# Loading q and k once, on the two partition halves of one tile, and filling the other operand planes by DMAs within SBUF

## The chip, the cores and the metric

The kernel runs on one core of one Trainium2 chip. The metric is the device time of one execution in microseconds, from the core's own records; it is quoted as the median of several executions. The core has TensorE (PE, matmuls, with its weight loads PEld), VectorE (DVE), ScalarE (ACT), GpSimd (POOL) and SyncE (SP), which issues nearly all DMAs here and runs each queue in order.

## The reference

Two layers follow each other, in float32 throughout.

```python
# attention: B=8, H=8, S=576, D=64
scores = matmul(q, k.T) / sqrt(D)
cum = cumsum(log(clip(f, 1e-4, 1)), axis=-1)
scores = where(causal, -1e9, scores + cum[:, None] - cum[None, :])
attn = exp(scores - max) / (sum + 1e-9)
x = matmul(attn, v)                     # reshaped to 4608 tokens x 512
# feed forward: 512 -> 2048 -> 512
h = x @ w_in
out = (max(h, 0) + log1p(exp(-|h|))) @ w_out
```

Matmuls of float32 operands are costly, so most of them are made from operands that are split in two: a rounded part ("hi", type fp32r) and the rest ("lo"). A product is then hi·hi + hi·lo + lo·hi.

## The kernel before, in words

The work is 68 attention jobs and ten feed-forward blocks of tokens (two of 256, eight of 512). Jobs 0 to 11 belong to the first batch and use unsplit float32 operands (the "plain" path, `load32`). Jobs 12 to 67 are 56 heads, eight for each of the other seven batches, and use split operands; only they are touched by the change. While attention runs, feed-forward matmuls of blocks that are ready are put between its matmuls; when the last head is done, about 200 us of feed-forward are left.

The order of the instructions of each engine is written by a planner (`Plan`, L48). It holds estimated costs and latencies of every operation, places the one that can start first, picks an engine where two are allowed (`copies`, L194: ACT or DVE; `scales`, L199: DVE, ACT or POOL), and emits it. Each engine, and SP's queue, then runs its list in that order on the chip and waits where an operand is late. Buffers come from pools with a fixed number each (`BUFS`, L252).

For one head of the split path:

- `load` (L669): two DMAs (L673) bring q and k, transposed to 64 partitions, into the tile `raw`, once on partitions 0 to 63 and once on 64 to 127. Each DMA carries both q and k, 288 KB. There is one `raw` buffer, so the load of a head waits until the head before has done with it.
- `prepare` (L694) fills `T`, a tile of four planes of 576 columns. There are two of them; a head's `T` comes free when the scores of the head two before it are done.
  - plane 0: q hi, on both halves (`q_hi`, a cast at L211)
  - plane 1: q lo on the lower half (`q_lo`, L718), constants and decay rows above it
  - plane 2: k hi on the lower half, k lo on the upper (`k_hi`, a cast at L211; `k_lo`, L712)
  - plane 3: k hi on the lower half (`k_hi2`, a DMA within SBUF, L709), constants and decay rows above it
  - the decay rows come by two small DMAs from DRAM (L702, L703)
- scores (L756, L757): for each of six pieces, one matmul of plane 0 by plane 2 over 128 partitions (q hi·k hi and q hi·k lo at once) and one of plane 1 by plane 3 over 68 partitions (q lo·k hi and the decay).
- then the row minimum with the mask (DVE, L761), the exponential (ACT, L781), the reciprocal of the sum (DVE, L794), the scaling of the weights (`scale`, L803 on ACT, L805 on POOL or DVE), the transposes (PE, L852), the split of the weights (L211 and L871) and the product with v (PE, L911).

Of the kernel before, what the change touches and what calls it, by code (L numbers as in the profile page):

```python
# [12 lines left out]
F32R = mybir.dt.float32r  # L13
# [34 lines left out]
class Plan:  # L48
# [120 lines left out]
def on_act(n, more=0.0, psum=False):  # L169
    return On("ACT", (0.067 if psum else 0.095) + n / 1200 + more)  # L170
# [16 lines left out]
NO_ENGINE = On("", 0.0)  # L187
# [6 lines left out]
def copies(n):  # L194

    return [on_act(n), on_dve(n, True, bias=COPY_BIAS)]
# [8 lines left out]
def subs(n):  # L205

    return on_dve(n, port=True)


def copy(e, out, in_):  # L210
    (e.tensor_copy if hasattr(e, "tensor_copy") else e.copy)(out, in_)  # L211
# [3 lines left out]
def tile_decay_attention_softplus_ffn(  # L215
# [18 lines left out]
    B, D, H, _, S = qkT.shape  # L234
    NT, DM = out.shape
    DFF = w_in.shape[1]
    P = 128
# [7 lines left out]
    BH = B * H  # L245
# [4 lines left out]
    QF, QR = [(0, 128), (128, 128)], [(256, 64), (320, 128), (448, 128)]  # L250

    BUFS = dict(T=2, att=4, h=2, acc=2, fe=4, ph=3, pl=3, ph64=2, gh=LAG + 1, gl=LAG + 1, xh=1, xl=1,  # L252
                x32=2, wl=2, vhl=3, vraw=1, raw=1)
    plan = Plan(BUFS | dict(T0=4, stat=4, p=2, xh0=1, xh1=1, xl0=1))
    add, give = plan.add, plan.give

    def add_dma(emit, kb, n=1, eng="SP", **more):
        return add(on_dma(kb, n, eng), emit, lag=dma_lag(kb, n, eng), **more)
# [9 lines left out]
    def buf(tag, shape, name, dtype=F32):  # L268
        return pool.tile(shape, dtype, tag=tag, name=name, bufs=BUFS[tag])
# [9 lines left out]
    T = {}  # L279
# [79 lines left out]
    def decay():  # L359
        box = {}  # L360

        def load(e):
            box["f"] = buf("wl", [P, 1024], "fs")[0:BH, 0:S]
            e.dma_start(out=box["f"], in_=f)

        def clip(e):
            e.tensor_scalar(box["f"], box["f"], 1e-4, 1.0, ALU.max, ALU.min)

        def log(e):
            e.activation(box["f"], box["f"], AF.Ln)  # L370

        def scan(e):

            c = cum[0] = buf("x32", [P, NCC, S], "cum")[0:BH, 0, :]
            x = box["f"][:, 0:256]
            e.tensor_tensor_scan(c[:, 0:256], x, x, 0.0, ALU.add, ALU.min)

        def scan_rest(e):
            c = cum[0]
            x = box["f"][:, 256:S]  # L380
            e.tensor_tensor_scan(c[:, 256:S], x, x, c[:, 255:256], ALU.add, ALU.min)

        def split(e):
            hl = buf("raw", [P, 2, S], "chl", F32R)
            ch, cl = box["hl"] = hl[0:BH, 0, :], hl[0:BH, 1, :]
            e.tensor_copy(ch, cum[0])
            e.tensor_sub(cl, cum[0], ch.bitcast(F32))

        def store(e):
            for r in range(2):  # L390
                e.dma_start(out=aug_d[:, r, :], in_=box["hl"][r].bitcast(F32))

        o = add_dma(load, BH * S / 256, takes=("wl",))
        o = add(on_dve(S, True), clip, after=[o])
        l = add(on_act(S), log, after=[o])
        decay_ready["first"] = add(On("DVE", 0.63), scan, after=[l], takes=("x32",))
        c = decay_ready["sums"] = add(On("DVE", 0.78), scan_rest, after=[decay_ready["first"]])
        give("wl", [c])
        def rest(after):
            s = add(On("DVE", 1.05, 0.0, True), split, after=[c, *after], takes=("raw",))  # L400
            w = add_dma(store, BH * S / 128, 2, after=[s] + first_rows)
            give("raw", [add(NO_ENGINE, mark, after=[w])])
            decay_ready["rows"] = w
            cum_used.append(s)

        return rest
# [168 lines left out]
    def attention(job):  # L575

        b, heads = job["b"], job["heads"]
# [90 lines left out]

        def load():  # L669
            def qk(e):  # L670
                raw = buf("raw", [P, 2, S], f"raw{n}")
                for i in range(2):
                    e.dma_start(out=raw[64 * i : 64 * i + 64], in_=qkT[b, :, heads[0]])  # L673
                st["raw"] = raw[:, 0, :], raw[:, 1, :]

            st["qk"] = add_dma(qk, 576, 2, takes=("raw",))

        def split_v():
            def v_hi(e):
# [14 lines left out]
        def prepare():  # L694
            def begin(e):
                nonlocal t, tb, qA, qB, kA, kB
                t = T[number % 2]
                tb = t.bitcast(F32)
                qA, qB, kA, kB = (t[:, i, :] for i in range(4))

            def decay_rows(e):
                e.dma_start(out=tb[64:66, 1, qs:qe], in_=aug_d[bh][:, qs:qe])  # L702
                e.dma_start(out=tb[66:ST, 3, :], in_=aug_d[bh])  # L703

            def k_hi(e):
                copy(e, t[:, 2, :], st["raw"][1])

            def k_hi2(e):
                e.dma_start(out=tb[0:64, 3, :], in_=tb[0:64, 2, :])  # L709

            def k_lo(e):
                e.tensor_sub(t[top, 2, :], st["raw"][1][top], tb[top, 2, :])  # L712

            def q_hi(e):
                copy(e, t[:, 0, qs:qe], st["raw"][0][:, qs:qe])

            def q_lo(e):
                e.tensor_sub(t[0:64, 1, qs:qe], st["raw"][0][0:64, qs:qe], tb[0:64, 0, qs:qe])  # L718

            split_v()  # L720
            if number < nplain + 2:
                set_rows(number % 2, T0_end[2 * (number % 2)] + T0_end[2 * (number % 2) + 1])
            start = add(NO_ENGINE, begin, after=T_set[number % 2], takes=("T",), lag=0.0)
            a = add_dma(decay_rows, 9, 2, after=[start, decay_ready["rows"]])
            kh = add(copies(S), k_hi, after=[start, st["qk"]])
            qh = add(copies(qe - qs), q_hi, after=[start, st["qk"]])
            kh2 = add_dma(k_hi2, 144, after=[kh])
            kl = add(On("DVE", 0.79, 0.0, True), k_lo, after=[kh])
            ql = add(subs(qe - qs), q_lo, after=[qh])
            give("raw", [kl, ql])  # L730
            st["T"] = [a, kl, ql, kh2]


        def stat_tile(ti):
# [236 lines left out]
        def loads():  # L971
# [5 lines left out]
            s=[lambda ti=ti: stat_tile(ti) for ti in range(nt)],  # L977
            w=[lambda bi=bi: weights(bi) for bi in range(len(banks))],
# [485 lines left out]
```

## Time and profile before

| | before |
|---|---|
| median of 3 runs | 1197.46 us (1197.27 to 1198.01) |
| span of the profiled execution | 1196.2 us |
| busy PE / PEld | 1177.1 / 969.0 us |
| busy DVE / ACT / POOL | 851.4 / 852.5 / 140.3 us |
| granted TensorE clock | 1.000 |
| moved by DMAs | 172.01 MB |
| scores of split heads run from / to | 135.3 / 988.4 us |

The span is read from the first to the last instruction of one execution; the median stands 1.26 us above it. A busy PE is not a PE at its peak, since its matmuls overlap and their ends are modelled: idle time that shows between them is a floor for what PE lost. The page's idle columns say how long an engine stood still just before a group of instructions, and what ended most of that.

### The profile page before, as it was taken

To read this page: it belongs to the slowest core of one execution; us is meant where nothing else is said; L and a number is where in the kernel's file an instruction comes from. 1 tells how busy PE (TensorE), PEld (TensorE's weight loads), DVE (VectorE), ACT (ScalarE), POOL (GpSimd) and SP (SyncE) were. 2 spreads that over 40 slices of the span, in tenths; PEclk is the share of its full clock that TensorE was granted. 3 is DMA by queue.
4 is the path that set the end of the run, shared out by engine and by line. 5 is a ranking of instruction groups with operands and counts; after the bars stand their busy time and mean duration, and the time that the engine had idled before them with its cause. 6 is when DMAs were issued, how large, how long until landed. Compare 5 with 4: busy or idle time off the path is not lost.

```text
span 1196.2 us, 19275 instructions
## 1 busy us (share of the span) xinstructions
PE 1177.1 (98%) x6122; PEld 969.0 (81%) x6122; DVE 851.4 (71%) x2085; ACT 852.5 (71%) x2033; POOL 140.3 (12%) x143
## 2 busy tenths in 40 slices
PE   8999999999999999999999999999999999999998
PEld 6666678878888888888888888888888888888887
DVE  7998999897787778777787778677867773223322
ACT  6676888888886778678777778688867773444543
POOL 3200011111111110102011101011111110000000
PEclk9999999999999999999999999999999999999999
DMA  7855655545555645655565546555465524211210
GB/s 215 255 171 162 183 152 155 131 135 155 143 160 166 177 131 147 182 162 155 143 187 158 147 130 187 149 162 147 146 181 151 156 81 136 89 36 53 88 53 35
DMA packets 107317, 172.01 MB, mean 144 GB/s; under 512 B 20256, under 2 KB 77616, under 8 KB 107216
## 3 DMA queue, kind: packets, MB, share of 16 engines
q1 hardware_dynamic: 107200, 170.78, 50.1%
q8 instruction: 48, 0.79, 0.3%
q14 instruction: 53, 0.43, 0.1%
q10 hardware_dynamic: 16, 0.01, 0.0%
HBM read 126.49 MB, written 35.95 MB: 136 GB/s over the span
## 4 chain that ended last, share of the span: by engine, by line
PE 77%; DVE 12%; ACT 4%; DMA 3%; issue 2%; POOL 1%; SPq 0%; DVEq 0%; POOLq 0%; ACTq 0%
PE h L1069 27%; PE acc L1154 27%; PE b L852 7%; PE o L911 5%; PE s L756 3%; PE s L757 3%; DVE s L761 2%; PE h L1050 2%; PE acc L1173 1%; POOL p L805 1%; ACT p L781 1%; DMA raw<-in_qkT 1%; PE s L754 1%; PE o L905 1%; DVE T L712 1%
## 5 line engine op out<-in xcount | busy, mean ns | idle before, releaser
L1069 PE MATMUL h<-xh,wih 128*128 128x512 f32 (+1 forms) x576 | 229.1, 401 | 0.0
L781 ACT ACTIVATE p<-s,negm 128x288 f32<-128x288 f32 (+7 forms) x384 | 182.6, 478 | 55.0 <-DVE negm L761 53.4
L1069 PE MATMUL h<-xl,wih 128*128 128x512 f32 (+1 forms) x576 | 216.8, 379 | 0.0
L805 POOL TENSOR_SCALAR p<-p,rsum 64x64 f32<-64x64 f32 (+4 forms) x106 | 119.1, 1133 | 742.9 <-DVE rsum L794 292.5
L1116 DVE SCALAR_TENSOR_TENSOR h<-h,e 128x512 f32<-128x512 f32 x136 | 95.1, 699 | 138.1 <-ACT e L1108 137.3
L761 DVE CUSTOM_DVE_ANT_0 s<-s,cmask 128x288 f32<-128x288 f32 (+5 forms) x320 | 137.2, 439 | 74.1 <-PE s L757 63.6
L1102 ACT ACTIVATE e<-h 128x512 f32<-128x512 f32 x144 | 85.4, 594 | 112.7 <-PE h L1069 106.8
L1154 PE MATMUL acc<-woh_dt_float32r,gh 128*128 128x512 f32 x376 | 153.1, 407 | 0.1
L1069 PE MATMUL h<-xh,wl 128*128 128x512 f32 (+1 forms) x576 | 148.6, 380 | 0.0
L1154 PE MATMUL acc<-woh_dt_float32r,gl 128*128 128x512 f32 x376 | 147.3, 392 | 0.0
L1154 PE MATMUL acc<-wol_dt_float32r,gh 128*128 128x512 f32 x376 | 147.0, 391 | 0.0
L871 DVE TENSOR_TENSOR pl<-b,ph 128x512 fp32r<-128x512 f32 x168 | 110.8, 664 | 29.5 <-ACT ph L211 27.5
L211 ACT CAST ph<-b 128x512 fp32r<-128x512 f32 (+2 forms) x180 | 88.6, 500 | 50.8 <-PE b L852 47.4
L1069 PEld LDWEIGHTS h<-xh,wl 128*128 128x128 f32 x576 | 104.9, 188 | 21.5
L1069 PEld LDWEIGHTS h<-xh,wih 128*128 128x128 f32 x576 | 108.8, 189 | 15.5 <-PE b L852 0.2
L1069 PEld LDWEIGHTS h<-xl,wih 128*128 128x128 f32 x576 | 108.9, 189 | 14.7 <-DVE xl L1021 0.4
L852 PE MATMUL b<-ident,p 128*128 128x128 f32 (+1 forms) x728 | 117.8, 270 | 2.6 <-DVE x L940 0.6
L1124 DVE TENSOR_TENSOR gl<-h,gh 128x512 fp32r<-128x512 f32 x136 | 93.5, 687 | 36.6 <-ACT gh L211 36.0
L211 ACT CAST gh<-h 128x512 fp32r<-128x512 f32 x117 | 68.6, 586 | 53.6 <-DVE h L1116 48.1
L803 ACT ACTIVATE p<-p,rsum 128x320 f32<-128x320 f32 (+7 forms) x190 | 97.4, 573 | 5.1 <-DVE rsum L794 4.6
L756 PE MATMUL s<-T 128*64 128x64 f32 x336 | 98.5, 304 | 1.5 <-ACT p L781 1.3
L852 PEld LDWEIGHTS b<-ident,p 128*128 128x128 f32 (+1 forms) x728 | 86.1, 138 | 16.4 <-ACT p L781 2.1
(154 smaller groups left out, 2293.6 us busy)
## 6 DMA issues: line engine op xcount, KB each, us to landing
wl<-wil_d SPq DMA_DIRECT2D x72, 512.0 KB
raw<-in_qkT SPq DMA_DIRECT2D x112, 288.0 KB
g_d<-gh SPq DMA_DIRECT2D x84, 128.0 KB
g_d<-gl SPq DMA_DIRECT2D x84, 128.0 KB
vr<-in_vR SPq DMA_DIRECT2D x64, 160.0 KB
out<-ob SPq DMA_DIRECT2D x36, 256.0 KB
T<-T SPq DMA_DIRECT2D x56, 144.0 KB
sto<-in_w_out SPq DMA_DIRECT2D x11, 512.0 KB
```

What stands on the lines that cost most here:

```text
L211: (e.tensor_copy if hasattr(e, "tensor_copy") else e.copy)(out, in_)
L756: e.matmul(o, qA[:, q0:end], kA[:, a:z], start=True, stop=False)
L761: e.tensor_tensor_reduce(out=box["o"], in0=box["o"], in1=cmask[0:n_q, right - w : right], scale=-0.125, scalar=m0 if i else 3.0e38, op0=AL ...
L781: e.activation(o, box["o"], AF.Exp, bias=m1, scale=-1.0, accum_out=acc)
L803: e.activation(a, a, AF.Copy, scale=f_)
L805: e.tensor_scalar(a, a, f_, None, ALU.mult)
L852: e.transpose(box["ps"][0 : x.shape[1], at : at + one.shape[1]], x, one)
L871: e.tensor_sub(box["l"], box["ps"][:, 0:w], box["h"].bitcast(F32))
L1069: e.matmul(o, l, r, start=m == 0, stop=m == 11)
L1116: e.scalar_tensor_tensor(h, h, 0.0, box["e"], ALU.max, ALU.add)
L1124: e.tensor_sub(box["l"], box["t"], box["h"].bitcast(F32))
L1154: e.matmul(st["acc", tt], l, r[fc], start=first and m == 0, stop=last and m == 2,)
```

## The change

q is loaded to partitions 0 to 63 and k to 64 to 127 of one `raw` tile of one plane, 144 KB each; there are two `raw` buffers of half the size. One cast (`hi`) rounds both, into plane 0, and one subtraction (`lo`) makes both remainders, into plane 2. Four DMAs within SBUF, 144 KB each, then put the parts where the matmuls want them, in place of one:

1. after `hi`: k hi from the upper half of plane 0 to the lower half of plane 3
2. after `lo`: q lo from the lower half of plane 2 to the lower half of plane 1
3. after 2: k hi from the upper half of plane 0 to the lower half of plane 2
4. after 1, 3 and `lo`: q hi from the lower half of plane 0 to its upper half

A head's scores wait for 4 and for the decay rows. The matmuls and what they compute stay as they were. The split of the cumulated decay of all heads, done once early on, borrowed the `raw` buffer as one tile of two planes and now takes both as two tiles.

```diff
-                x32=2, wl=2, vhl=3, vraw=1, raw=1)
+                x32=2, wl=2, vhl=3, vraw=1, raw=2)
...
-            hl = buf("raw", [P, 2, S], "chl", F32R)
-            ch, cl = box["hl"] = hl[0:BH, 0, :], hl[0:BH, 1, :]
+            ch, cl = box["hl"] = [buf("raw", [P, S], f"c{x}", F32R)[0:BH] for x in "hl"]
...
             def qk(e):
-                raw = buf("raw", [P, 2, S], f"raw{n}")
+                st["raw"] = buf("raw", [P, S], f"raw{n}")
                 for i in range(2):
-                    e.dma_start(out=raw[64 * i : 64 * i + 64], in_=qkT[b, :, heads[0]])
-                st["raw"] = raw[:, 0, :], raw[:, 1, :]
-
-            st["qk"] = add_dma(qk, 576, 2, takes=("raw",))
+                    e.dma_start(out=st["raw"][64 * i : 64 * i + 64], in_=qkT[b, :, heads[0], i])
+
+            st["qk"] = add_dma(qk, 288, 2, takes=("raw",))
...
-            def k_hi(e):
-                copy(e, t[:, 2, :], st["raw"][1])
-
-            def k_hi2(e):
-                e.dma_start(out=tb[0:64, 3, :], in_=tb[0:64, 2, :])
-
-            def k_lo(e):
-                e.tensor_sub(t[top, 2, :], st["raw"][1][top], tb[top, 2, :])
-
-            def q_hi(e):
-                copy(e, t[:, 0, qs:qe], st["raw"][0][:, qs:qe])
-
-            def q_lo(e):
-                e.tensor_sub(t[0:64, 1, qs:qe], st["raw"][0][0:64, qs:qe], tb[0:64, 0, qs:qe])
+            def hi(e):
+                copy(e, t[:, 0, :], st["raw"])
+
+            def lo(e):
+                e.tensor_sub(t[:, 2, :], st["raw"], tb[:, 0, :])
+
+            def move(to, i, of, j):
+                return lambda e: e.dma_start(out=tb[to, i, :], in_=tb[of, j, :])
+
+            low = slice(0, 64)
...
-            kh = add(copies(S), k_hi, after=[start, st["qk"]])
-            qh = add(copies(qe - qs), q_hi, after=[start, st["qk"]])
-            kh2 = add_dma(k_hi2, 144, after=[kh])
-            kl = add(On("DVE", 0.79, 0.0, True), k_lo, after=[kh])
-            ql = add(subs(qe - qs), q_lo, after=[qh])
-            give("raw", [kl, ql])
-            st["T"] = [a, kl, ql, kh2]
+            h_ = add(copies(S), hi, after=[start, st["qk"]])
+            l_ = add(On("DVE", 0.75, 0.0, True), lo, after=[h_])
+            give("raw", [l_])
+            k3 = add_dma(move(low, 3, top, 0), 144, after=[h_])
+            q1 = add_dma(move(low, 1, low, 2), 144, after=[l_])
+            k2 = add_dma(move(low, 2, top, 0), 144, after=[q1])
+            q0_ = add_dma(move(top, 0, low, 0), 144, after=[k2, k3, l_])
+            st["T"] = [a, q0_]
```

The planner writes new lists from this, so instructions move on every engine. Two places matter below.

On SP's queue, where heads 13 and 14 are prepared (`T1` and `T0` are their tiles, `aug_d` the decay rows, `wil_d` low parts of w_in on their way to DRAM, `vr` the load of v), the list before was:

```order
L614 DMA vr12_1353<-in_vR 128x320
L618 DMA vr12_1353<-in_vR 64x64 x2
L673 DMA raw14_1376<-in_qkT 64x1152 x2
L504 DMA wil_d_102<-wil9_1386 128x2x256
L702 DMA T0_1099<-aug_d_104 2x576
L703 DMA T0_1099<-aug_d_104 2x576
L614 DMA vr13_1433<-in_vR 128x320
L618 DMA vr13_1433<-in_vR 64x64 x2
L709 DMA T0_1099<-T0_1099 64x576
```

and is now:

```order
L711 DMA T1_1327<-T1_1327 64x576 x2
L504 DMA wil_d_102<-wil9_1377 128x2x256
L673 DMA raw15_1415<-in_qkT 64x576 x2
L614 DMA vr13_1430<-in_vR 128x320
L618 DMA vr13_1430<-in_vR 64x64 x2
L711 DMA T1_1327<-T1_1327 64x576
L701 DMA T0_1104<-aug_d_104 2x576
L702 DMA T0_1104<-aug_d_104 2x576
L711 DMA T0_1104<-T0_1104 64x576 x2
L711 DMA T1_1327<-T1_1327 64x576
L614 DMA vr14_1483<-in_vR 128x320
```

The load of q and k stands a head further ahead (head 15 where it was head 14), and the last move of head 13 stands behind the decay rows and two moves of head 14, which wait for the end of head 12's scores.

On POOL, the scaling of the weights of four heads in a row in a middle batch (`rsum0` to `rsum3` belong to four heads in turn, the last figure is the width of the piece) was:

```order
L805 TENSOR_SCALAR p0_64_91<-p0_64_91,rsum0_87 64x64
L805 TENSOR_SCALAR p0_256_92<-p0_256_92,rsum0_87 128x192
L805 TENSOR_SCALAR p0_640_95<-p0_640_95,rsum0_87 128x576
L805 TENSOR_SCALAR p1_384_98<-p1_384_98,rsum1_88 128x320
L805 TENSOR_SCALAR p0_384_93<-p0_384_93,rsum2_89 128x320
L805 TENSOR_SCALAR p1_64_96<-p1_64_96,rsum3_90 64x64
L805 TENSOR_SCALAR p1_640_100<-p1_640_100,rsum3_90 128x576
```

and is now:

```order
L801 TENSOR_SCALAR p0_64_91<-p0_64_91,rsum0_87 64x64
L801 TENSOR_SCALAR p0_256_92<-p0_256_92,rsum0_87 128x192
L801 TENSOR_SCALAR p1_384_98<-p1_384_98,rsum1_88 128x320
L801 TENSOR_SCALAR p0_384_93<-p0_384_93,rsum2_89 128x320
L801 TENSOR_SCALAR p1_256_97<-p1_256_97,rsum3_90 128x192
L801 TENSOR_SCALAR p1_512_99<-p1_512_99,rsum3_90 128x448
```

The widest pieces, 576 columns, have left POOL for ACT and DVE: over the whole program POOL's scalings go from 106 to 82, and those 576 wide from 26 to 3.

More of the change, by code (lines that the diff above doesn't have):

```diff
@@ L399, in rest @@
         def rest(after):
-            s = add(On("DVE", 1.05, 0.0, True), split, after=[c, *after], takes=("raw",))
+            s = add(On("DVE", 1.05, 0.0, True), split, after=[c, *after], takes=("raw", "raw"))
             w = add_dma(store, BH * S / 128, 2, after=[s] + first_rows)
-            give("raw", [add(NO_ENGINE, mark, after=[w])])
+            for _ in range(2):
+                give("raw", [add(NO_ENGINE, mark, after=[w])])
             decay_ready["rows"] = w
```

## The prediction

> **What bounds the kernel now.** I read the page first, then busy time by stage, then the chain of waits inside the stages where PE was not full.
>
> ```profile
> span 1196.2 us, 19275 instructions
> PE 1177.1 (98%) x6122; PEld 969.0 (81%) x6122; DVE 851.4 (71%) x2085; ACT 852.5 (71%) x2033; POOL 140.3 (12%) x143
> PE 77%; DVE 12%; ACT 4%; DMA 3%; issue 2%; POOL 1%; SPq 0%; DVEq 0%; POOLq 0%; ACTq 0%
> ```
>
> PE is busy for 98% of the span, and 77% of the chain that ended last is PE. The change removes no matmul, so it can only win where the other 23% of that chain lies. The windows show where (engine busy us and instructions, clock, DMA share, GB/s):
>
> ```profile
> core 0: us, PE busy (x) PEld busy (x) DVE busy (x) ACT busy (x) POOL busy (x), PEclk, DMA share, GB/s
> 135.00:260.00 125.00, 120.05 (x734) 99.76 (x733) 115.13 (x306) 104.88 (x277) 18.22 (x15) 1.00 0.53 141
> 260.00:900.00 640.00, 636.53 (x3393) 537.54 (x3392) 490.07 (x1208) 495.14 (x1211) 87.98 (x79) 1.00 0.56 158
> 900.00:990.00 90.00, 89.43 (x475) 75.64 (x474) 67.54 (x160) 70.79 (x168) 11.99 (x11) 1.00 0.47 134
> 1000.00:1100.00 100.00, 100.00 (x448) 83.06 (x447) 26.23 (x39) 41.21 (x68) 0.00 (x0) 1.00 0.22 70
> ```
>
> From 135 to 260 us, the first eleven split heads, DVE is busy for 92% (115.13 of 125) and PE stands idle for 4.95 us. From 260 to 990 us PE is idle for 3.47 + 0.57 = 4.04 us of 730, with DVE at 77%. After that only feed-forward is left and PE is full. What the change touches ends before 990 us, and a microsecond of PE idle time removed there shortens the end by a microsecond, because the feed-forward left over just starts earlier. So 4.95 + 4.04 = 9.0 us is what shows to be won; the real stalls can be somewhat larger, since matmul ends are modelled and short waits hide in them.
>
> **The change, part by part.** These are the operations it removes, over the whole program (busy us, mean ns, idle before, releaser):
>
> ```profile
> L211 ACT CAST T<-raw 128x576 fp32r<-128x576 f32 x81 | 52.0, 672 | 14.2 <-PE s L756 7.9 <-DMA raw<-in_qkT 4.5 <-DMA T<-aug_d 1.7
> L211 DVE CAST T<-raw 128x576 fp32r<-128x576 f32 x31 | 14.1, 456 | 2.5 <-DMA raw<-in_qkT 1.2 <-DMA T<-aug_d 1.1
> L718 DVE TENSOR_TENSOR T<-raw,T 64x576 fp32r<-64x576 f32 x56 | 43.0, 767 | 0.8
> L712 DVE TENSOR_TENSOR T<-raw,T 64x576 fp32r<-64x576 f32 x56 | 42.3, 755 | 1.8
> ```
>
> Two casts and two subtractions a head become one of each. A subtraction over 128 partitions has the same 576 columns as the two over 64 (L871 runs 512 columns on 128 partitions in 687 ns, so width, not partitions, sets it), so the new one takes 0.755 us. Over 56 heads DVE loses about 42.5 us of subtractions, and DVE and ACT together 56 casts, 0.456 to 0.672 us each: 26 to 38 us.
>
> ```profile
> L871 DVE TENSOR_TENSOR pl<-b,ph 128x512 fp32r<-128x512 f32 x112 | 77.0, 687 | 26.4 <-ACT ph L211 25.1
> ```
>
> *Term 1, the early stage.* Eleven heads are prepared between 135 and 260 us. DVE is freed of 11 x 0.76 = 8.4 us there. A second thing goes: the wait for the one `raw` buffer. Around head 21:
>
> ```profile
> 223.38 1.18 SPq L673 DMA_DIRECT2D raw<-in_qkT  x2
> ...
> 225.02 0.30 PE L757 MATMUL s<-T 68*128 68x288 f32 x1
> ...
> 228.49 0.83 DVE L211 CAST T<-raw 128x576 fp32r<-128x576 f32 x2 [1.12 <-DMA T<-aug_d]
> 228.97 0.49 SPq L709 DMA_DIRECT2D T<-T  x1
> 229.72 0.75 DVE L712 TENSOR_TENSOR T<-raw,T 64x576 fp32r<-64x576 f32 x1
> ...
> 232.54 0.74 DVE L718 TENSOR_TENSOR T<-raw,T 64x576 fp32r<-64x576 f32 x1
> ```
>
> and, from the chain of waits (start us, us, what), a load's and a small DMA's time from issue to landing:
>
> ```profile
> 235.44 4.47 DMA raw<-in_qkT
> ...
> 250.79 1.48 DMA T<-aug_d
> ```
>
> `T` was free when head 19's last score ended (225.32), but the casts ran at 228.49: the second load was issued near 223.97, and 4.47 us, the landing time that the chain of waits shows for such a load, end at 228.44. (The timeline names the decay rows, which landed then too; the casts do not read them.) The load could not go earlier because it waited for the last subtraction of the head before. In this stage ACT and DVE stood still for 4.5 + 1.7 + 1.2 + 1.1 = 8.5 us before these casts (the four DMA releasers in the rows above). With two buffers and the load a head ahead on SP's list this goes; the load also halves, to 144 KB.
>
> What is that worth? Nothing, if the freed time is not what PE waits for. At most 8.4 + 2.3 = 10.7 us (the subtractions, and DVE's own part of those waits), if DVE alone sets the pace of the stage. PE's visible idle time, 4.95 us, lies between. DVE at 92% is near to setting the pace, but part of PE's idle time ends with ACT or POOL, so I take 3.0 us.
>
> *Term 2, the ends of batches.* Later PE is idle mostly in a few places a batch apart. One piece of the chain:
>
> ```profile
> 864.30 0.20 DVE rsum L794
> ...
> 864.68 3.86 POOL p L805 x2
> ...
> 868.58 0.74 PE b L852 x5
> ```
>
> and two windows of ten microseconds with such a place, and the two rows of the widest pieces:
>
> ```profile
> 731.00:741.00 10.00, 9.33 (x51) 7.72 (x52) 8.38 (x25) 7.92 (x21) 3.41 (x2) 1.00 0.59 177
> 860.00:870.00 10.00, 8.87 (x49) 7.29 (x49) 8.29 (x25) 7.83 (x21) 3.85 (x2) 1.00 0.56 176
> L805 POOL TENSOR_SCALAR p<-p,rsum 128x576 f32<-128x576 f32 x26 | 46.8, 1800 | 0.0
> L803 ACT ACTIVATE p<-p,rsum 128x576 f32<-128x576 f32 x36 | 27.5, 763 | 0.0
> ```
>
> The sums are ready, POOL scales two pieces one after the other in 3.86 us, and the transposes wait; PE loses 1.13 us of those ten and 0.67 of the ten around 736. The wide piece takes 1.80 us on POOL and 0.76 on ACT. In the new order 23 of the 26 wide pieces have left POOL, since ACT and DVE have room. Nothing to be won if PE then waits for the next thing (a subtraction of DVE), all 4.04 us if every idle moment there was of this kind. Seven batches at 0.2 us: 1.5 us.
>
> *Term 3, the longer way to a ready T.* Before, `T` was complete after casts, one DMA and the subtractions side by side. Now cast (0.67), subtraction (0.755) and three DMAs follow each other. No row shows how long a move takes to land. A load of 4.5 KB took 1.48 us and one of 288 KB 4.47 (above), so a move of 144 KB lies between; by size, half way, 2.9 us. Then T is ready 0.1 + 0.67 + 0.755 + 3 x 2.9 = 10.2 us after it came free, and 6 or 14.9 us at the ends of the bounds. What covers it is PE's work between the last score of the head two before and the first of this one. The shortest such stretch before is head 20's:
>
> ```profile
> 215.59 0.30 PE L757 MATMUL s<-T 68*128 68x288 f32 x1
> ...
> 227.99 0.19 PE L756 MATMUL s<-T 128*64 128x64 f32 x1
> ...
> 240.14 0.19 PE L756 MATMUL s<-T 128*64 128x64 f32 x1
> ...
> 569.65 0.30 PE L757 MATMUL s<-T 68*128 68x288 f32 x1
> ...
> 591.22 0.19 PE L756 MATMUL s<-T 128*64 128x64 f32 x1
> ```
>
> From 215.89 to 227.99 that is 12.1 us; head 21's (225.32 to 240.14) is 14.8, and head 43's in the steady part (569.95 to 591.22) 21.3. So at 2.9 us the chain is hidden with 1.9 us to spare, and the term is 0. Without that cover each microsecond late stalls PE, since PE runs its list in order.
>
> The price of a move in the skill: the Trainium skill, "DMA: Bandwidth & Descriptors", section "Anatomy of one DMA", gives about 2.0 us fixed and the bytes at 436 GB/s, so an estimate of 2.3 us; "SBUF — State Buffer", "Door 1: The DMA port swizzle", says that 64 partitions reach only half of the ports, which speaks against moves of this shape and makes it 2.7. By either the chain is 8.5 to 9.6 us and the term still 0; the sum is the same.
>
> *Term 4, queues.* SP issues 168 DMAs more, 0.49 us each (L709 above): 1.5 us a head in periods of 12 us and more. What stands behind a waiting move on SP (the next q and k, v, w_in's low parts) is late by as much as the move waits; the planner set other DMAs between the moves, so I count 0. The bytes grow by 144 KB a head (loads 576 to 288, moves 144 to 576), 8 MB of 172, on DMA engines 47 to 56% busy: 0.
>
> The sum is 3.0 + 1.5 = 4.5 us. The profiled execution would take 1196.2 - 4.5 = 1191.7 us; the median stands 1.26 above its span, so 1193.0.
>
> **The rivals.** *More is won*: DVE alone holds the early stage, and the stalls hidden in modelled ends go too. 10.7 + 4.0 give 1182.8 as the extreme, about 1187 as a likely one. DVE's 92% speaks for it; ACT's 84% (104.88 of 125) and the waits for POOL speak against.
>
> *Nothing reaches PE*: helper engines get idle time, and PE, which has other matmuls in its list, waits for the next thing instead. 1197, give or take 1. PE's 98% speaks for it, the stage at 92% DVE against.
>
> *The chain of moves takes the place of the wait*: a move lands later than 3.5 us, because SP's queue holds it behind something or the DMA engines are busy. From there on 0.1 + 0.67 + 0.755 + 3 x 3.5 = 12.0 reaches the 12.1 us of the shortest stretch and PE stalls at the first score. At 4.0 us the chain is 13.5, 1.4 us over, at some eight heads of the early stage: 11 us lost, 4.5 won, 1204. The 4.47 of a load speaks for it, and the last move of head 13 behind head 14's on SP; that the load carries twice the bytes and came from HBM speaks against. That four 64-partition moves per head press on half of the ports (the page above) adds to its chance.
>
> **How the numbers follow.** About 0.2% (2.4 us) is what a measurement of this kernel can tell from no change. The forecast, 2.4 to 8 us faster, has 0.47; more than that 0.11; nothing reaches PE 0.22; the chain of moves 0.20. So faster 0.58, same 0.22, slower 0.20. The range takes in the likely end of the first rival, 1187, and reaches to 1201, half way into the last.
>
> **What would show it.** Right: in 135 to 260 us DVE below 90% and PE idle under 2.5 us; no ACT or DVE wait before the casts that a load of q and k ends; POOL pieces of the batch ends shorter than 3 us; no PE wait that a DMA into `T` ends. Wrong: PE or its weight loads waiting at the scores for a DMA of `T` (the third rival), or DVE freed with PE's idle time unchanged (the second).

## The result, and the profile after

The changed kernel takes 1190.16 us (median of 4 runs, 1187.36 to 1190.59); the kernel before, on the same chip, 1197.74 us (1197.27 to 1199.2). The ratio is 0.9929, with a 95% interval of 0.9917 to 0.9941: 7.6 us faster. The profiled execution has a span of 1188.8 us, 7.4 us under that of before.

The page of the changed kernel, span, engines (busy us, share, instructions) and the chain that ended last:

```profile
span 1188.8 us, 19425 instructions
PE 1172.2 (99%) x6122; PEld 968.3 (81%) x6122; DVE 819.2 (69%) x2039; ACT 829.4 (70%) x1991; POOL 111.3 (9%) x119
PE 90%; DVE 6%; DMA 2%; issue 1%; ACT 1%; SPq 0%; DVEq 0%
```

PE's share of the chain went from 77% to 90%. DVE lost 32.2 us of work, ACT 23.1, POOL 29.0.

The operations on q and k that are left (busy us, mean ns, idle before, releaser), and the wide scalings that POOL kept:

```profile
L708 DVE TENSOR_TENSOR T<-raw,T 128x576 fp32r<-128x576 f32 x56 | 42.2, 754 | 0.0
L211 ACT CAST T<-raw 128x576 fp32r<-128x576 f32 x53 | 35.5, 670 | 7.3 <-PE s L752 4.7 <-DMA raw<-in_qkT 2.4
L211 DVE CAST T<-raw 128x576 fp32r<-128x576 f32 x3 | 1.4, 455 | 0.0
L801 POOL TENSOR_SCALAR p<-p,rsum 128x576 f32<-128x576 f32 x3 | 5.2, 1719 | 0.0
```

The subtraction over 128 partitions takes 754 ns, as the two over 64 did one by one (755 and 767). The 2.4 us of ACT's idle time that end with a load of q and k all lie behind the early stage. The windows by stage, and the two stretches of ten microseconds at the ends of batches that the prediction showed (engine busy us and instructions, clock, DMA share, GB/s):

```profile
135.00:260.00 125.00, 121.32 (x750) 101.91 (x748) 108.00 (x300) 104.34 (x275) 15.42 (x14) 1.00 0.60 157
260.00:900.00 640.00, 638.25 (x3417) 541.66 (x3417) 471.24 (x1183) 484.61 (x1200) 66.09 (x60) 1.00 0.60 169
900.00:990.00 90.00, 89.32 (x469) 74.99 (x469) 64.10 (x154) 67.00 (x161) 8.89 (x8) 1.00 0.45 135
731.00:741.00 10.00, 10.00 (x60) 8.76 (x59) 7.81 (x22) 6.94 (x21) 1.23 (x2) 1.00 0.71 214
860.00:870.00 10.00, 9.07 (x53) 7.63 (x53) 7.56 (x23) 6.88 (x18) 1.72 (x2) 1.00 0.71 209
```

In the early stage (135 to 260 us) DVE fell from 92% to 86%, but PE's idle time only from 4.95 to 3.68 us. From 260 to 990 us PE's idle time fell from 4.04 to 2.43 us.

Where the time came from is read best off the scores, which every variant computes in the same order. The first score of the thirteenth split head, and the last score of all, in the kernel before:

```profile
286.41 0.19 PE L756 MATMUL s<-T 128*64 128x64 f32 x1
...
988.51 0.30 PE L757 MATMUL s<-T 68*128 68x288 f32 x1
```

and in the changed kernel:

```profile
283.90 0.19 PE L752 MATMUL s<-T 128*64 128x64 f32 x1
...
981.09 0.30 PE L753 MATMUL s<-T 68*128 68x288 f32 x1
```

So 2.5 us are won by the thirteenth head, 4.9 us in the heads after it (702.1 us between these two rows became 697.2), and nothing in the feed-forward behind. The thirteenth is a good place to cut: in the kernel before no cast waits for a load of q and k behind it. Between the two scores PE runs the same matmuls in both. The windows from the one to the other, before and then after:

```profile
286.40:988.80 702.40, 698.93 (x3723) 590.38 (x3721) 534.38 (x1313) 541.72 (x1324) 98.22 (x89) 1.00 0.55 155
```

```profile
283.90:981.40 697.50, 695.93 (x3723) 590.18 (x3721) 511.94 (x1277) 526.35 (x1298) 71.02 (x65) 1.00 0.58 165
```

Of the 4.9 us, 1.9 are PE's idle time (3.47 to 1.57). The other 3.0 are in its busy time: the same 3723 matmuls, kind by kind, count 698.93 us before and 695.93 after. So this part is most likely waiting that the modelled ends book as work. Where it lies shows when each matmul is counted from its own start to the start of the next one. The 660 transposes of this stretch then took 60.6 us before and 57.3 after, the 420 matmuls that read hidden values loaded back from DRAM (`g_d`) 100.9 and 99.5, and all others together 540.6 and 540.3. What PE and its weight loads waited for before the transposes, in the kernel before from 265 to 980 us, was POOL's scaling:

```profile
PE b L852 <- POOL p L805: 1.3, 3, 0.8
PEld b L852 <- POOL p L805: 2.7, 4, 1.1
```

In the change no such wait is left there. The longest wait of its PE behind 260 us is a new one, at a score:

```profile
PE s L752 <- PE acc L1150: 0.9, 1, 0.9
```

The profile names PE itself, whose matmul had long been done. By the semaphore updates in the trace, a move within this head's `T` landed 0.09 us before the score began at 869.38 us, 5.6 us after it was issued. It is the idle time that the row of 860 to 870 us shows.

### The profile page after: what moved, and what is told of

Read it like the earlier page. It is cut to its first block, busy times and chain, and to the rows that moved or that the text cites. A ratio compares the mean times of both kernels' runs of the same rounds, so it can differ in the third digit from the quotient of the medians.

```text
span 1188.8 us, 19425 instructions
## 1 busy us (share of the span) xinstructions
PE 1172.2 (99%) x6122; PEld 968.3 (81%) x6122; DVE 819.2 (69%) x2039; ACT 829.4 (70%) x1991; POOL 111.3 (9%) x119
## 4 chain that ended last, share of the span: by engine, by line
PE 90%; DVE 6%; DMA 2%; issue 1%; ACT 1%; SPq 0%; DVEq 0%
PE h L1065 31%; PE acc L1150 30%; PE b L848 8%; PE o L907 7%; PE s L752 4%; PE s L753 3%; PE h L1046 2%; PE acc L1169 2%; PE o L901 1%; PE s L750 1%; DVE s L757 1%; DMA sti<-in_w_in 1%; DVE xl L1017 1%; DVE pl L867 0%; DVE woh_dt_float L450 0%
## 5 line engine op out<-in xcount | busy, mean ns | idle before, releaser
L801 POOL TENSOR_SCALAR p<-p,rsum 128x448 f32<-128x448 f32 (+4 forms) x82 | 90.4, 1110 | 762.5 <-DVE rsum L790 319.9
L211 ACT CAST ph<-b 128x512 fp32r<-128x512 f32 (+2 forms) x168 | 82.0, 490 | 43.4 <-PE b L848 37.4
L799 ACT ACTIVATE p<-p,rsum 128x192 f32<-128x192 f32 (+7 forms) x201 | 100.5, 556 | 8.3 <-DVE rsum L790 8.0
```

The costliest lines, as they stand in the source:

```text
L799: e.activation(a, a, AF.Copy, scale=f_)
L801: e.tensor_scalar(a, a, f_, None, ALU.mult)
```

## The experiments

All are variants of the kernel before or of the change. The table has what each measured, the kernel before beside it (1197.05 to 1197.5 us as a median in three groups of runs, 1197.74 beside the change), and, from each profile, PE's idle time and DVE's busy time from 135 to 260 us, with the idle time of ACT and DVE there that a load of q and k ended.

| kernel | median us | ratio, 95% interval | PE idle | DVE busy | waits for loads |
|---|---|---|---|---|---|
| before | 1197.5 | | 4.95 | 115.1 | 5.7 |
| the change (two raw buffers) | 1190.2 | 0.9917–0.9941 | 3.68 | 108.0 | 0 |
| one_raw | 1186.0 | 0.9891–0.9918 | 0.42 | 113.0 | 0 |
| short_chain | 1189.1 | 0.9917–0.9942 | 3.30 | 110.1 | 0 |
| raw1_short | 1186.3 | 0.9896–0.9923 | 0.77 | 115.7 | 0 |
| after_plan576 | 1186.5 | 0.9894–0.9921 | 0.86 | 110.3 | 0 |
| raw1_plan576 | 1190.0 | 0.9925–0.9950 | 1.31 | 112.7 | 0 |
| raw1_engines | 1189.3 | 0.9919–0.9944 | 0.93 | 118.3 | 0 |
| busy_again | 1192.1 | 0.9943–0.9970 | 3.56 | 117.5 | 0 |
| raw1_busy | 1195.7 | 0.9979–0.9996 | 3.66 | 116.1 | 2.7 |
| raw1_twice | 1192.1 | 0.9941–0.9966 | 4.85 | 109.0 | 3.3 |
| no_qlo | 1189.2 | 0.9922–0.9950 | 2.91 | 114.9 | 1.0 |
| before_plan288 | 1203.7 | 1.0035–1.0063 | 6.98 | 114.1 | 6.1 |
| narrow_pool | 1204.1 | 1.0044–1.0069 | 4.88 | 118.1 | 4.4 |

### Is it the second raw buffer? (one_raw)

```diff
-                x32=2, wl=2, vhl=3, vraw=1, raw=2)
+                x32=2, wl=2, vhl=3, vraw=1, raw=1)
...
-            ch, cl = box["hl"] = [buf("raw", [P, S], f"c{x}", F32R)[0:BH] for x in "hl"]
+            hl = buf("raw", [P, 2, S], "chl", F32R)
+            ch, cl = box["hl"] = hl[0:BH, 0, :], hl[0:BH, 1, :]
...
-                st["raw"] = buf("raw", [P, S], f"raw{n}")
+                st["raw"] = buf("raw", [P, 2, S], f"raw{n}")[:, 0, :]
```

> The changed kernel with one raw buffer instead of two: loads of half the size, one cast, one subtraction and four moves stay, but a head's load waits again for the subtraction of the head before. The theory that the freed operations of VectorE and ScalarE made the gain (relief) expects 1190 to 1192 us, since the load now lands in less time and the casts wait little. The rival, that the load a head ahead made it (prefetch), expects 1194 to 1197, with VectorE and ScalarE waiting again before the casts between 135 and 260 us.

Measured: 1186.02 us (1185.69 to 1186.35), 4 us faster than the change and below both expected ranges. Its early stage, the first score of the thirteenth head and the last score:

```profile
135.00:260.00 125.00, 124.58 (x770) 105.13 (x768) 112.99 (x305) 105.95 (x281) 19.66 (x16) 1.00 0.61 163
...
279.90 0.19 PE L752 MATMUL s<-T 128*64 128x64 f32 x1
...
976.17 0.30 PE L753 MATMUL s<-T 68*128 68x288 f32 x1
```

The load now has to wait for the head before again, and yet in this stage no cast waits for it: with 144 KB instead of 288 KB, and the buffer free after one subtraction instead of two, the load has landed before `T` is free. The second buffer is not what won. Nor is it what costs 4 us, as the last two runs show.

### Is it the engine time? (busy_again, raw1_busy, raw1_engines)

Three ways to give ACT, DVE and POOL their work back: a cast and a subtraction more for each head. On `raw` itself, in the change (busy_again) and in the variant with one buffer (raw1_busy):

```diff
+            def hi2(e):
+                copy(e, st["raw"].bitcast(F32R), st["raw"])
+
+            def lo2(e):
+                e.tensor_sub(st["raw"], st["raw"], st["raw"])
...
-            give("raw", [l_])
+            h2 = add(copies(S), hi2, after=[l_])
+            l2 = add(On("DVE", 0.75, 0.0, True), lo2, after=[h2])
+            give("raw", [l2])
```

> The changed kernel with the removed engine time put back: after the subtraction one more cast and one more subtraction over the same 576 columns, in place in raw, whose results nothing uses and for which no score waits. Relief expects the gain to be gone: 1196 us or more, with pieces of 576 columns back on GpSimd. Prefetch expects 1190 to 1192.

> The change with one raw buffer (which took 1186.0 us), and with a cast and a subtraction more for each head, both 128 x 576 and in place on the loaded q and k after the real ones: ACT, DVE and POOL get back the work that the change removed, while nothing that T is made of waits for the added ones (only the raw buffer does, which the next load waits for). Relief theory (the engines' freed time is the gain): it loses most of what one_raw won on the kernel before, so 1193 us or more. Load theory (the smaller load, which lands earlier, is the gain): the added operations hold the one buffer 1.2 to 1.4 us longer, so it loses about as much as the casts come later, 1188 to 1191. Order theory (the planner happened to write better lists): anything from 1184 to 1195, without relation to DVE's busy time. In the first run of this kind, on two buffers, 2 us of 7 were lost; the same here would be 1188.

And on a tile of their own (raw1_engines), so that neither `raw` nor `T` is held by them:

```diff
+            def hi2(e):
+                st["spare"] = buf("spare", [P, S], f"spare{n}", F32R)
+                copy(e, st["spare"].rearrange("p (x s) -> p x s", x=2), cmask[:, 0 : S // 2].unsqueeze(1).to_broadcast([P, 2, S // 2]))
+
+            def lo2(e):
+                e.tensor_sub(st["spare"], st["spare"].bitcast(F32), st["spare"].bitcast(F32))
...
+            h2 = add(copies(S), hi2, after=[l_])
+            add(On("DVE", 0.75, 0.0, True), lo2, after=[h2])
```

> The change with one raw buffer (1186.0 us), and for each head a cast and a subtraction more, 128 x 576 each, on a tile of their own that nothing else reads: the engines get back the work that the change removed, but neither the raw buffer nor T is held by it. The same two operations on raw itself gave 1195.65, and the same lists with loads of double bytes gave 1192.1. Relief theory (engine time is the gain): 1193 to 1196 again. Load theory (what counts is when q and k land, which the operations on raw delayed by holding the buffer): 1186 to 1189. Both in part: 1190 to 1192.

Measured: busy_again 1192.07 us (2 us over the change, at the edge of what prefetch expected), raw1_busy 1195.65 us (9.6 over one_raw; the relief theory's range, and more than the load theory had allowed), raw1_engines 1189.26 us (3.2 over one_raw, between the load theory's range and that of both in part). The early stage of raw1_engines, first, and then its first score of the thirteenth head and its last score:

```profile
135.00:260.00 125.00, 124.07 (x768) 104.80 (x768) 118.25 (x318) 107.25 (x282) 23.81 (x18) 1.00 0.59 161
...
280.52 0.19 PE L760 MATMUL s<-T 128*64 128x64 f32 x1
...
979.55 0.30 PE L761 MATMUL s<-T 68*128 68x288 f32 x1
```

DVE is busy for 118.25 of 125 us, 95% and more than before the change, and PE stands idle for 0.93 us. So DVE's share of busy time does not set the pace of this stage. (The added operations are not on the way to `T`, as those that the change removed were.) What differs in raw1_busy is that the added operations hold the one buffer, and there the casts wait for the load again:

```profile
ACT T L211 <- DMA raw<-in_qkT: 2.2, 1, 2.2
...
DVE T L211 <- DMA raw<-in_qkT: 0.5, 1, 0.5
```

Against one_raw raw1_busy loses 6.1 us by the thirteenth head and 3.9 behind it; that its lists are new has a part in this which was not measured. raw1_engines loses 0.6 us by the thirteenth head and 2.8 us behind it, where the transposes go from 57.6 us in one_raw to 59.0 and matmuls wait for POOL's scaling again (0.7 us). So what engine time is worth lies in the later batches. Its size, about 3 us here, is no more than new lists alone are worth (below).

### Is it the load? (raw1_twice)

The variant with one buffer, where each load brings its half twice, 288 KB again, into the two planes of a tile of the old size; the second plane isn't read. The planner's price stays, so every engine's list is that of one_raw, operation by operation.

```diff
-                st["raw"] = buf("raw", [P, 2, S], f"raw{n}")[:, 0, :]
+                raw = buf("raw", [P, 2, S], f"raw{n}")
                 for i in range(2):
-                    e.dma_start(out=st["raw"][64 * i : 64 * i + 64], in_=qkT[b, :, heads[0], i])
+                    kq = qkT[b, :, heads[0], i].unsqueeze(1).to_broadcast([64, 2, S])
+                    e.dma_start(out=raw[64 * i : 64 * i + 64], in_=kq)
+                st["raw"] = raw[:, 0, :]
```

> The change with one raw buffer (1186.0 us), each of its two loads carrying its half twice, 288 KB each as before the change, into the two planes of a tile of the old size (the second plane is not read). The planner is not told, so every engine's list is that of one_raw, operation by operation: only the loads' bytes and landing time differ. Load theory: the casts start about 1.5 us later in the early stage and the gain over the kernel before mostly goes, 1191 or more. Relief theory: what was freed on the engines stays freed, so 1186, at most 1188. Order theory: 1186.

Measured: 1192.11 us, some 6 us over one_raw with the same lists. The early stage, ACT's and DVE's waits for loads there, and the two scores:

```profile
135.00:260.00 125.00, 120.15 (x737) 100.73 (x736) 108.95 (x294) 102.12 (x268) 19.37 (x16) 1.00 0.73 180
...
ACT T L211 <- DMA raw<-in_qkT: 2.9, 3, 1.7
ACT T L211 <- DMA vr<-in_vR: 1.5, 1, 1.5
...
DVE T L211 <- DMA raw<-in_qkT: 0.4, 1, 0.4
...
284.52 0.19 PE L754 MATMUL s<-T 128*64 128x64 f32 x1
...
983.60 0.30 PE L755 MATMUL s<-T 68*128 68x288 f32 x1
```

The waits are back, and PE's idle time is as long as in the kernel before (4.85 against 4.95 us), though DVE is less busy than in one_raw. But it is idle at another place. PE's waits in that stage:

```profile
PE s L754 <- PE acc L1171: 1.4, 2, 0.7
PE s L754 <- issue: 1.3, 1, 1.3
PE s L754 <- DMA T<-T: 0.9, 2, 0.6
PE s L754 <- PE o L909: 0.8, 1, 0.8
```

All six of these stand before a head's scores, and each ended about 0.1 us after a move within `T` had landed: the late load makes the chain of moves late, and PE waits for `T`. In the kernel before, the waits of PE that the profile lists in this stage are for ACT, DVE and POOL, and none is for a DMA. So this run shows what bytes are worth to the new kernel, and not what the old loads cost the old one.

By the semaphore updates in the trace, a load of 288 KB lands some 4.4 us after its issue (median of the 96 that can be told), one of 144 KB in one_raw some 3.0. A move within `T` took 2.75 us in the median against 2.45 in one_raw, so the bytes press on other DMAs too. 4.6 us of the loss come by the thirteenth head. 2.8 come later, 2.1 of them at the matmuls that read hidden values loaded back from DRAM (100.4 us against 98.3) and none at the transposes (57.6 in both). The two make 7.4, since the profiled execution was 1 us slower than the median. This is the cleanest of the runs: nothing but the loads' bytes differs, and with them their landing and what they press on other DMAs (the DMA engines' share in the row rose from 0.61 to 0.73).

### Relief without the new loads (no_qlo)

The kernel before without the subtraction that makes q's low part.

```diff
+            if j == 1:
+                e.memset(T[i].bitcast(F32)[0:64, j, :], 0.0)
...
-            ql = add(subs(qe - qs), q_lo, after=[qh])
-            give("raw", [kl, ql])
-            st["T"] = [a, kl, ql, kh2]
+            give("raw", [kl, qh])
+            st["T"] = [a, kl, qh, kh2]
```

> The kernel before without the subtraction that makes q's low part (56 operations of 755 ns on DVE, 42 us); plane 1's lower half is set to zero once instead, so the product q lo by k hi is left out of the scores' value while its matmuls run as before. Loads, buffers and the one move stay those of before. Relief theory: nearly the same DVE time is freed as by the change, and T is ready sooner as well, so it wins as much as the change or more, 1186 to 1191. Load theory: the gain is in the load, so 1194 to 1197. Order theory: lists are written anew, so 1190 to 1197 without a rule.

Measured: 1189.23 us, 8.3 us under the kernel before. It is what the relief theory asked for, but does not prove it: without that subtraction the one `raw` buffer is free sooner, and the waits for loads in the early stage fell from 5.7 to 1.0 us:

```profile
ACT T L211 <- DMA raw<-in_qkT: 1.0, 1, 1.0
```

Its first score of the thirteenth head comes at 283.06 us, 3.35 us earlier than before. In this stage freed time and freed buffer can't be told apart. Behind the thirteenth head they can: there no cast of the kernel before waited for a load, the loads of no_qlo are the old ones of 288 KB, and it still wins 5.4 us (702.1 became 696.7), more than the change does there. The transposes take 57.7 us instead of 60.6. This is the relief theory's range, which the load theory's (1194 to 1197) did not allow; the lists are new here too.

### POOL's wide scalings (narrow_pool)

The kernel before, with 576-wide scalings kept off POOL.

```diff
-                st["norm"].append(add(scales(ends[ti], not plain), scale, after=[r]))
+                st["norm"].append(add(scales(ends[ti], not plain and ends[ti] < S), scale, after=[r]))
```

> The kernel before, with one edit: pieces of the weights that are 576 wide may be scaled on ScalarE or VectorE only, never on GpSimd. If the wide pieces on GpSimd were what the transposes at the ends of batches waited for, this alone wins a part: 1193 to 1196 us, with PE idle time from 260 to 990 us down from 4.0 to about 1.5. If they only took the place of work that the other two engines had no time for, 1197 us or more.

Measured: 1204.12 us, 7 us slower than before. No wait of PE behind 260 us ends with POOL any more, and the heads became longer all the same. The ten microseconds around 865, and what PE waited for from 260 to 990 us:

```profile
860.00:870.00 10.00, 8.92 (x49) 7.19 (x48) 9.81 (x24) 8.14 (x21) 0.00 (x0) 1.00 0.40 121
```

```profile
PE b L852 <- DVE x L940: 2.7, 5, 0.7
PE s L756 <- DVE pl L871: 1.3, 4, 0.4
```

POOL does nothing there, DVE is busy for 9.81 of the ten, and PE, as idle as before (8.92 busy against 8.87), waits for DVE instead of POOL. Behind the thirteenth head the transposes did get shorter (60.6 to 58.3 us), but the scores got longer by more (72.1 to 78.2). At the ends of batches the helper engines together are short, and POOL's pieces were their overflow. That is the place where freed engine time can count; moving the pieces without freeing time only moves the wait.

### The length of the chain of moves (short_chain, raw1_short)

Two of the four moves leave the chain; `T` is complete after two in a row instead of three. The same edit on two buffers (short_chain) and on one (raw1_short):

```diff
-            k2 = add_dma(move(low, 2, top, 0), 144, after=[q1])
-            q0_ = add_dma(move(top, 0, low, 0), 144, after=[k2, k3, l_])
-            st["T"] = [a, q0_]
+            q0_ = add_dma(move(top, 0, low, 0), 144, after=[k3, l_])
+            k2 = add_dma(move(low, 2, low, 3), 144, after=[q1, k3])
+            st["T"] = [a, q0_, k2]
```

> The changed kernel with a shorter chain of moves: k hi goes to plane 2 from plane 3 (after moves 1 and 2), and q hi goes to the upper half of plane 0 after move 1, so two moves stand behind the subtraction instead of three. If the chain is hidden as forecast, the time stays within 1 us of the change (1189 to 1191). If it still costs something between 135 and 260 us, where the last move now ends 1 to 3 us ahead of the first score, 1186 to 1189.

> The change with one raw buffer (1186.0 us), and with two of the four moves taken out of the chain: q hi waits for plane 3 and the subtraction alone, and plane 2's k hi comes from plane 3 after plane 1's move has read plane 2, so T is ready after two moves in a row instead of three. If the length of the chain costs something: 1183 to 1185. If it is covered, as the forecast said: 1186, give or take 1.5 for another order. On two buffers the same edit gave 1189.1 against 1190.2.

Measured: 1189.06 and 1186.29 us, beside 1190.2 and 1186.0 for the chain of three. One move less is worth between 1.1 us won and 0.3 lost: nothing that shows. The chain is covered, but not everywhere: the change has the one wait of 0.9 us above, and short_chain one of 1.5 us at a score at 207.96 us, 0.09 us behind the landing of a move that took 5.9 us. one_raw and raw1_short have none.

### What a new order alone is worth (before_plan288, after_plan576, raw1_plan576)

In all three only the planner's price for the two loads is changed: 288 KB for 576 in the kernel before, 576 for 288 in the change and in one_raw. The operations are the same as in their parent; some hundreds of PE's 6122 matmuls stand elsewhere in its order, and a few casts and scalings are on another of ACT, DVE and POOL (ACT has 2033 instructions before and 2021 in before_plan288).

```diff
-            st["qk"] = add_dma(qk, 576, 2, takes=("raw",))
+            st["qk"] = add_dma(qk, 288, 2, takes=("raw",))
```

> The kernel before, where only the planner's price for the two loads of q and k is halved (288 KB for 576): the operations are the same on the chip, their order differs in places (about 134 of 5258 rows on PE). It measures what a new order alone is worth. Order theory (a new list may be worth as much as the change): 3 us or more off 1197.5, either way. The other theories: within 1.5 us of it.

> The change itself (two raw buffers, 1190.2 us), where only the planner's price for the loads is the old one, 576 KB. If the 4 us between two buffers and one are order: somewhere from 1185 to 1192, and as likely near 1186 as near 1190. If the second buffer itself costs: 1190 give or take 1.5.

> The change with one raw buffer (1186.0 us), where only the planner's price for the loads is the old one, 576 KB. If one buffer is itself better: 1186 give or take 1.5, and below the run of the same price on two buffers. If 1186.0 was a lucky order: 1188 to 1191.

Measured: 1203.71 us (6.4 over the kernel before), 1186.52 us (3.6 under the change), 1189.96 us (3.9 over one_raw). With either price, two buffers gave 1190.2 and 1186.5, one gave 1186.0 and 1190.0. So the number of buffers makes no difference that can be told from order, and 1186.0 is partly a lucky list. The early stages of before_plan288 and of after_plan576:

```profile
135.00:260.00 125.00, 118.02 (x715) 98.17 (x714) 114.13 (x305) 96.22 (x256) 16.50 (x15) 0.99 0.48 134
```

```profile
135.00:260.00 125.00, 124.14 (x766) 104.36 (x766) 110.30 (x299) 104.96 (x279) 18.52 (x16) 1.00 0.59 160
```

and the chain of waits of before_plan288 in that stage (start us, us, what):

```profile
138.93 4.37 DMA raw<-in_qkT
...
193.07 4.90 DMA raw<-in_qkT
...
205.83 5.29 DMA raw<-in_qkT
...
229.94 4.91 DMA raw<-in_qkT
```

Here the planner believed in a shorter load; the loads took as long as ever. All of the 6.1 us of waits before the casts are now ACT's (in the kernel before 4.5 of 5.7), and PE's transposes waited 3.5 us for ACT's exponentials, which they did not in the kernel before. The waits for loads themselves hardly grew (5.7 to 6.1 us), so that they are what cost the 6.4 us is argued from the chain, where in the kernel before such a load stands three times in this stage, and not shown. Of the 6.4 us, 6.1 are lost by the thirteenth head. The other two prices moved the time by 3.6 us down and 3.9 up with no wait for a load in any of the four early stages, so loads are not all that an order changes.

## Why the prediction was right, and where it was not

The forecast was 1193.0 us with a range of 1187 to 1201; 1190.2 lies in it, and faster was the likeliest case. The steps one by one:

*Term 1, the early stage, 3.0 us.* 2.5 us came by the thirteenth head: the size held, its reason half. Of the two parts, the subtractions and the waits for the one `raw` buffer, the runs speak for the second. The waits before the casts are gone in this stage, as the prediction said they would be (2.4 us of such waits came up later, where there had been none). But "DVE at 92% is near to setting the pace" fell: raw1_engines has DVE at 95% and PE idle for 0.93 us. And the waits went for another cause than the prediction gave ("with two buffers and the load a head ahead"): one buffer does as well. Twice the bytes bring them back (raw1_twice, 3.3 us), and so does a buffer held for longer (raw1_busy, 2.7 us). How much was to be had was under-estimated: one_raw wins 6.5 us by the thirteenth head, more than the 4.95 us of idle time that showed.

Why the change itself won only 2.5 of these shows in its own waits in that stage, of PE and of DVE, and in the chain there:

```profile
PE b L848 <- DVE pl L867: 2.0, 2, 1.3
...
DVE gl L1120 <- DMA wil_d<-wil: 2.7, 1, 2.7
```

```profile
175.51 3.96 DMA wil_d<-wil
...
179.49 0.69 DVE gl L1120
180.18 0.60 DVE pl L867
```

A store of a low part of w_in to DRAM, issued shortly behind two loads of q and k and a store of the output, took 3.96 us; DVE waited for its `gl` buffer, the next split of the weights came late, and PE waited 1.3 us for that (the longest of the row above). Neither one_raw nor after_plan576 has such a wait there. So PE's idle time did not fall under 2.5 us as the prediction asked. That it is a matter of which DMA stands where, and not of two buffers, follows from after_plan576; that the transfers ahead of the store are what slowed it is argued, not shown.

*Term 2, the ends of batches, 1.5 us.* The place and the mechanism were right and the size was not: 4.9 us came, more than its upper bound of 4.04, which was PE's visible idle time. The prediction had said that the real stalls are larger than what shows, and then took the visible sum as the bound: 3.0 of the 4.9 us stood in PE's busy time. 3.3 us of it came at the transposes, where PE's wait for POOL's scaling ended, as the term said (POOL busy for 1.72 us in the ten around 865 against 3.85 before). The freed engine time is what allows this: no_qlo, with the old loads, wins 5.4 us here; raw1_engines, with the work put back on engines alone, loses 2.8; and narrow_pool, which takes the pieces from POOL and frees nothing, lost 7 us in all. 1.4 us more came at matmuls that read hidden values loaded back from DRAM. raw1_twice loses time at those and not at the transposes, so that part may be the smaller loads; in the pair itself it is not shown. The exact sizes can't be told from what a new order does.

*Term 3, the chain of moves, 0.* Right in size, except for one place. The prediction's own sign against it, a score that waits for a DMA into `T`, came once, for 0.9 us at 869.38 us, which is as much as the change loses against one_raw behind the thirteenth head (697.2 and 696.3 us). The move took 5.6 us there, more than the 4.47 that the prediction had as its upper bound; four loads of 256 KB had been issued in the 3.1 us ahead of it. In raw1_twice, where the load is late, the same wait came six times. The chain from a free `T` on was reckoned as if the load had always landed by then, which holds for loads of 144 KB. The 2.9 us for a move was a fair size: the moves of the change took 2.5 us from issue to landing in the median (of the 201 of 224 that can be told), a quarter of them over 3.6. The Trainium skill's figures, 2.3 us as an estimate from "DMA: Bandwidth & Descriptors", section "Anatomy of one DMA — SWDGE (gpsimd) path" (which is written for another kind of queue than the one these moves ran on), and 2.7 with half of the ports ("SBUF — State Buffer", "Door 1: The DMA port swizzle"), lie on either side of that median; the quickest moves took 2.2, so this trace does not need the half-speed ports.

*Term 4, queues and bytes, 0.* By sum it did not turn the result, but the wait for the store above is of this kind, and it took 1.3 us of PE's time in the early stage; it was not looked for, since only SP's list and the engines' mean load were weighed.

*The rivals.* "Nothing reaches PE" did not come. "The chain of moves stalls PE" came at one score of the change, far from the eight that it was priced at. "More is won" did not come in the change, but in one_raw and after_plan576, which lie at 1186 to 1186.5, a little under its 1187.

Two figures of the prediction differ slightly from its own rows, and nothing hangs on them: DVE's share from 260 to 990 us is 76% and not 77, and the subtractions saved come to 43.0 us and not 42.5 (43.1 were saved).

One thing the prediction left out altogether: that new lists alone move the time. Nearly identical work in another order gave 1197.5 and 1203.7 before the change, and 1190.2 and 1186.5 behind it. The sign held in every pair that was run: each of the six kernels with the change's work in full, its chain of moves long or short (1186.0 to 1190.2), is faster than either order of the kernel before. Its size, 7.6 us, is one draw: from these kernels the same comparison could have given 7 to 18, so where in its range the forecast was met is in part luck. By place, 2.5 us of it came in the early stage, where the waits for loads went, and 4.9 in the later batches, where the waits for POOL went. How much of each is the new order stays open. For one_raw, with its lists held, twice the bytes cost some 6 of its 11.0 us, but by making PE wait for `T`, which the kernel before did not do; so this is no share of those 11.0 us. A kernel before whose planner is told the true landing time of its loads wasn't tried.

The fastest of the kernels is one_raw, 1186.0 us, 11.0 us under the kernel before in its group of runs.

## What to carry to other kernels

An engine at 92 or 95% need not be what paces a stage: look for what it stands waiting for, in the order that its list has, before counting its freed time as a gain. Ask this stage by stage, since the answer can differ: here the early stage lost time before loads and the later batches behind a full set of helper engines. Where lists are written ahead from estimated times, a transfer that lands a microsecond later than believed can hold up everything behind its reader. When the profile names an engine that had long been done, look for the DMA that landed just before. And before a change of less than 1% is explained, time one more order of the same work, since here that alone moved 4 to 6 us.

## What the runs showed that was not expected

- Loads of 288 KB took 4.3 to 4.4 us from issue to landing in the median, by run, loads of 144 KB 2.9 to 3.4: half the bytes save some 1.3 us, not half the time.
- A transfer within SBUF of 144 KB (2.5 us) is only a little quicker than a load of the same size from DRAM (2.9 to 3.4).
- Single moves took up to 5.6 us in the change and 6.0 in one_raw, over twice the median. In the change one of them cost PE 0.9 us, in one_raw none did.
- PE's visible idle time was no bound on what could be won: 4.9 us came where 3.47 stood idle; the rest stood in PE's busy time.
- DVE was busy for 95% of a stage, and PE stood idle for only 0.93 of its 125 us.
